# Half-precision output products, and one index search per head instead of two, in a kernel that joins attention with product-key experts

## The chip, the cores and the metric

The kernel runs on one core of one Trainium2 chip. The metric is device time in microseconds, from a median of runs; before the change it is 1775.51 us (three runs, 1774.38 to 1776.06). Beside it stands one execution under the hardware profiler, from which all other times here are taken.

## The reference

The input x has 2048 tokens of 512 numbers. After a layer norm two branches are computed from the same rows and added to x.

```python
q = (xn @ wq).reshape(B, S, 32, 16)         # 32 heads of 16
k = xn @ wk; v = xn @ wv                    # one key and one value head for all
p = softmax(q @ k.T * 16 ** -0.5)
branch_a = concat_heads(p @ v) @ wo         # wo: 512 x 512

q = einsum("nd,dhc->nhc", xn, w_q)          # 32 heads, two halves of 128
s1 = einsum("nhd,ed->nhe", q[..., :128], k1)   # 64 scores of the first half
s2 = einsum("nhd,ed->nhe", q[..., 128:], k2)   # 64 scores of the second half
i1, i2 = the two best of s1, of s2          # by score, with their places
top_s, top_e = the two best of the four sums s1 + s2; expert = 64 * i1 + i2
g = softmax(top_s)
act = gelu(einsum("nd,nhkd->nhk", xn, u[top_e]))
branch_b = einsum("nhk,nhk,nhkd->nd", g, act, v[top_e])
out = x + branch_a + branch_b
```

## The kernel before

The work is written out by hand, engine by engine, in one long order. A start of some 110 us norms and transposes x, forms queries, keys and values of the attention, and splits the weights into a half-precision number and a half-precision remainder, so that one product of single precision becomes three half-precision ones (high by high, high by low, low by high; the list is `TERMS`). Then 256 steps follow, `d` = 0 to 255. A step is eight score products, four exponentials on ACT (line 458) and 16 products with the values (line 468) of the attention; into its gaps a generator, `score_thread`, puts the other branch, and a planner says how much.

The expert branch handles the 16 row tiles of 128 tokens in four groups of four. Groups 0 and 1 are *sparse*: for each of the 512 slots (tile, head and choice) POOL gathers 128 rows of u and v from memory (line 1194), DVE takes the dot product with xn (line 1206), ACT the tanh, and DVE adds the weighted row of v (line 1241). Groups 2 and 3 are *dense*: one-hot tables turn the chosen experts into gate matrices, and all 4096 experts are multiplied through on PE (lines 930 and 1072). Both need the search. An *item* is one tile of 128 tokens by four heads: twelve half-precision products (line 702) leave 512 scores in PSUM, eight half-heads of 64. For each half-head DVE finds the eight largest (line 715) and then their places (line 717, in the chip two instructions: a load of the eight values and the find). There are 128 items. Four items make a `batch`, which picks the two best sums, the expert numbers (on POOL, line 761 on) and the gates.

In time the order is: items of group 0 while the expert weights are made (`wp_make`: products, norms in `wp_factors`, transposes, splits), from step 0; items of two eighths of group 1 and of group 2, to about step 60; the one-hot tables of group 2 and its dense sums, to about step 130; the remaining items of group 1 and those of group 3, to about step 180; the tables and dense sums of group 3, to the end. The slots run beside all this.

Two numbers set the pace. Each piece of generator work states a cost in microseconds of PE (`UNIT` = 0.235 for a half-precision product), and a step runs the generator until the sum reaches its share of `FILL`. And `pos` counts slots: so many dot products may be done by a step, by a rate that depends on the stage (`dense_on`):

```python
aim = done0 + (FILL - done0) * (d + 1) / half if d < half else 1e6
pos += (2.5 if len(IDX) < NC * TPH else 2.3 if 0 <= d - since < 20 else 1.75, 0, 0.25, 1.5, 0.5)[dense_on[0]]
```

In the dense sums the rate is 2.6 up to step 191 and after that whatever remains, divided by the steps that remain.

The attention's result leaves like this. Every 16 steps a pair of units ends; its rows are divided by their sums (`pair_tail`, line 517) and kept as `on`. When four pairs of a query block are there, `block_out` multiplies 128 rows with wo: four single-precision products (line 568), then one DVE addition to the row's sum (line 572). It runs for three of the four query blocks, four row blocks each, at steps chosen by `out_ready`, and states a cost of 3.6. The last query block has code of its own at the end (`last_out_a`, `last_out_b`). wo is loaded before each query block by `load_wo`, into buffers lent for it. One guard stands between the start and the steps (line 384): each engine loads a flag and skips a slow path.

DMA transfers are issued by SP's queue in its order, but for the gathers, which POOL issues, and some of the last stores. Work of a step goes through lists: `on_act` puts a function into the next step's ACT work, `behind` what DVE does after it, `store` what SP issues in a later step.

## Time and profile before

| | us |
|---|---|
| median of three runs | 1775.51 |
| the profiled execution, whole | 1775.3 |
| its span, first to last instruction | 1773.3 |
| PE busy | 1687.8 (95%) |
| DVE busy | 1593.0 (90%) |
| ACT busy | 1329.7 (75%) |
| POOL busy | 680.2 (38%) |
| TensorE's granted clock, mean | 0.995 |

In rows of a timeline stand start, length, engine, line, operation, and the tiles as out<-in. An operation's length covers its latency; the next may start before it ends, so a rate is read from start to start. PE is the matrix engine, PEld its weight loads, SPq an instruction that SP's queue issues. A matrix product in single precision appears as two passes. In groups of instructions the columns after the bar are busy time, the mean of one in ns, and the idle time of the engine just before, with what ended it; in lists of waits they are total, times, and the longest.

### The profile page before, as it was taken

To read this page: it belongs to the slowest core of one execution; us is meant where nothing else is said; L and a number is where in the kernel's file an instruction comes from. 1 tells how busy PE (TensorE), PEld (TensorE's weight loads), DVE (VectorE), ACT (ScalarE), POOL (GpSimd) and SP (SyncE) were. 2 spreads that over 40 slices of the span, in tenths; PEclk is the share of its full clock that TensorE was granted. 3 is DMA by queue.
4 is the path that set the end of the run, shared out by engine and by line. 5 is a ranking of instruction groups with operands and counts; after the bars stand their busy time and mean duration, and the time that the engine had idled before them with its cause. 6 is when DMAs were issued, how large, how long until landed. Compare 5 with 4: busy or idle time off the path is not lost.

```text
span 1773.3 us, 35071 instructions
## 1 busy us (share of the span) xinstructions
PE 1687.8 (95%) x11070; PEld 597.5 (34%) x11070; DVE 1593.0 (90%) x6367; ACT 1329.7 (75%) x1793; POOL 680.2 (38%) x893
## 2 busy tenths in 40 slices
PE   7989998999998889999999999999998899999998
PEld 3433333333333333333333333333333333333332
DVE  7748898999999977999999999999999779999995
ACT  6467787877776988888988666666679877777774
POOL 1024454445542003444444445445520125455450
PEclk9999999999999999999999999999999999999999
DMA  7378879999773469999999977767544779999994
GB/s 272 120 251 313 273 267 309 303 323 336 256 257 103 158 220 280 330 334 337 332 338 360 357 264 240 236 222 230 177 126 137 235 235 330 327 311 345 321 311 146
DMA packets 257272, 470.97 MB, mean 266 GB/s; under 512 B 107316, under 2 KB 118596, under 8 KB 257084
## 3 DMA queue, kind: packets, MB, share of 16 engines
q0 software_dynamic: 73728, 268.47, 44.1%
q1 hardware_dynamic: 182940, 199.59, 34.7%
q8 instruction: 87, 1.43, 0.3%
q14 instruction: 101, 0.83, 0.1%
q10 hardware_dynamic: 416, 0.66, 0.1%
HBM read 407.36 MB, written 56.39 MB: 262 GB/s over the span
## 4 chain that ended last, share of the span: by engine, by line
PE 52%; DVE 30%; ACT 6%; issue 3%; DMA 1%; POOL 0%; SPq 0%; ACTq 0%; DVEq 0%; POOLq 0%
PE pv L468 16%; PE sc L451 9%; PE pout L1072 8%; PE pact L930 7%; DVE i L717 7%; PE psc L702 6%; DVE xa L1241 5%; DVE m L715 5%; DVE g L1206 4%; ACT pt L458 4%; DVE oh L988 3%; PE pwo L568 2%; PE pw L647 1%; DVE obs L991 1%; DVE obs L990 1%
## 5 line engine op out<-in xcount | busy, mean ns | idle before, releaser
L458 ACT ACTIVATE pt<-sc 128x1024 f32<-128x1024 f32 x1024 | 990.4, 1025 | 316.9 <-PE sc L451 269.8
L1194 POOL DMA_INDIRECT g<-in_uv_dram,idx x512 | 550.1, 1074 | 862.2 <-DVE xa L1241 395.3
L468 PE MATMUL pv<-pt,vaug 128*32 128x512 f32 x4096 | 495.0, 601 | 0.0
L1241 DVE SCALAR_TENSOR_TENSOR xa<-g,w,xa 128x512 f32<-128x512 f32 x512 | 374.0, 746 | 0.1
L702 PE MATMUL psc<-wk,xt 128*128 128x512 f16 x1536 | 356.4, 380 | 7.2 <-DVE wk L663 4.7
L451 PE MATMUL sc<-qa,kaug 64*128 64x512 f16 x2048 | 323.5, 383 | 36.3 <-ACT pt L458 29.5
L1206 DVE CUSTOM_DVE_ANT_0 g<-g,xa 128x512 f32<-128x512 f32 x512 | 334.6, 683 | 14.5 <-DMA g<-in_uv_dram,idx 14.2
L702 PEld LDWEIGHTS <-xt 128*128 128x128 f16 x1536 | 140.7, 98 | 204.1 <-issue 55.5
L451 PEld LDWEIGHTS <-kaug 64*128 64x128 f16 x2048 | 82.6, 94 | 373.9 <-issue 370.5
L717 DVE FIND_INDEX8 i<-m,psc 128x8 uint32<-128x64 f32 x1024 | 206.6, 224 | 0.0
L468 PEld LDWEIGHTS pv<-pt,vaug 128*32 128x32 f32 x4096 | 107.2, 109 | 253.5 <-issue 253.5
L930 PE MATMUL pact<-xt,wk 128*128 128x512 f16 x768 | 182.6, 383 | 0.0
L1072 PE MATMUL pout<-wk,wd 128*128 128x512 f16 x768 | 175.8, 379 | 0.0
L715 DVE MAX8 m<-psc 128x8 f32<-128x64 f32 x1024 | 146.2, 216 | 6.5 <-PE psc L702 6.2
L1072 PEld LDWEIGHTS <-wd 128*128 128x128 f16 x768 | 73.0, 98 | 92.6 <-issue 8.1
L930 PEld LDWEIGHTS <-wk 128*128 128x128 f16 x768 | 69.1, 98 | 99.9 <-issue 26.7
L988 DVE TENSOR_TENSOR oh<-io,tr 128x2048 f16<-128x2048 f16 x64 | 78.0, 1218 | 4.9 <-PE pg L1026 4.8
L717 DVE MATCH_VALUE_LOAD i<-m,psc 128x8 f32 x1024 | 74.3, 73 | 0.0
L761 POOL CAST fi<-i 128x64 f32<-128x64 uint32 x30 | 7.7, 257 | 145.6 <-DVE i L717 142.0
L1075 DVE SCALAR_TENSOR_TENSOR da<-pout,cols,da 128x512 f32<-128x512 f32 x72 | 53.0, 744 | 5.9 <-PE pout L1072 5.4
L1145 DVE SCALAR_TENSOR_TENSOR gy<-gy,pact 128x512 f32<-128x512 f32 x60 | 40.8, 680 | 17.3 <-ACT gy L1144 17.0
L880 DVE SCALAR_TENSOR_TENSOR wk<-rw,cols,wk 128x512 f16<-128x512 f32 x64 | 47.5, 745 | 6.9 <-ACT wk L877 6.9
(227 smaller groups left out, 1451.9 us busy)
## 6 DMA issues: line engine op xcount, KB each, us to landing
wk<-dw SPq DMA_DIRECT2D x96, 256.0 KB
wqt<-in_wqT_dram SPq DMA_DIRECT2D x32, 512.0 KB
un<-in_uv_dram SPq DMA_DIRECT2D x16, 1024.0 KB
ds<-wk SPq DMA_DIRECT2D x64, 256.0 KB
gates<-dg SPq DMA_DIRECT2D x64, 256.0 KB
wk<-ds SPq DMA_DIRECT2D x64, 256.0 KB
dg<-gst SPq DMA_DIRECT2D x14, 928.0 KB
dw<-wk SPq DMA_DIRECT2D x32, 256.0 KB
```

The source lines that it names most:

```text
L451: nc.tensor.matmul(p[:, b, :], kaug[o:o + 64, kc * P:(kc + 1) * P], QA[u][o:o + 64, i, :], start=True, stop=True)
L458: nc.scalar.activation(PT[u, kc, i], p, AF.Exp, scale=SCALE)
L468: nc.tensor.matmul(PV[u][32 * j:32 * j + 32, :], vaug[:, kc, :], pt[:, b, :], start=kc == 0, stop=kc == 15)
L702: nc.tensor.matmul(p, XT[kk][:, a, j * P:(j + 1) * P], WC[n_][kk][:, bb, :], start=n == 0, stop=n == 11)
L715: nc.vector.max(m8[:, jb, s, :], p[:, s * E:(s + 1) * E])
L717: nc.vector.max_index(i8[:, jb, s, :], m8[:, jb, s, :], p[:, s * E:(s + 1) * E])
L930: nc.tensor.matmul(p, us[:, a, k * P:(k + 1) * P], XT[k][:, c, :], start=n == 0, stop=n == 11)
L988: nc.vector.tensor_tensor(out=oa, in0=num(P), in1=bc(0, tb, P), op=OP.is_equal)
L1072: nc.tensor.matmul(p, wd[0][:, a, j * P:(j + 1) * P], vs[:, c, :], start=n == 0, stop=n == last)
L1194: nc.gpsimd.indirect_dma_start(out=gt, out_offset=None, in_=uv, in_offset=bass.IndirectOffsetOnAxis(ap=IDX[ph, c, ti][:, s:s + 1], axis=0))
L1206: nc.vector.tensor_tensor_reduce(u, u, XN[TPH * ph + ti], scale=1.0, scalar=0.0, op0=OP.mult, op1=OP.add, accum_out=a[:, i:i + 1])
L1241: nc.vector.scalar_tensor_tensor(acc, v, w[:, i:i + 1], acc, op0=OP.mult, op1=OP.add)
```

## The change

**One search per head.** The eight maxima are taken per half-head as before, the first halves first. But they are written into one row of 16 places per head, the second half's from place 6 on, over the two smallest of the first half. So places 0 to 7 hold the six best of the first half and the two best of the second, and one find over the head's 128 columns gives all eight places; for the second half 64 is taken off. If the place of one of the second half's two is below 64, an equal value stood in the first half, and the place is not the one wanted. POOL works that out per batch (`over`), DVE keeps the running maximum (`most`), and near the end it becomes a flag. The whole kernel is written into the program a second time, with the old search (`exact`), behind a branch on that flag.

**Output products from halves.** wo is loaded once more in step 48, its squares summed, scaled by a power of two and split into a half-precision high and low part in steps 50 to 57, and stored; `load_wo` reads these, of the same size in bytes, for three query blocks. `pair_tail` now also splits the pair's rows: the high part on ACT, the low part on DVE. `block_out` makes twelve half-precision products, and the addition to the row sum takes the factor along. The last query block stays in single precision.

**Norms of the expert weights.** `wp_factors` makes one product of four columns and sums them on DVE, where four products of one column were accumulated, and scales on DVE what ACT scaled.

**Slots and pace.** `FILL` is 937.2 and a block costs 2.7. The slots' rate is 2.6 for 2.5 and 2.05 for 1.75.

```diff
-FILL = 948.0
+FILL = 937.2
...
+        nc.vector.tensor_scalar(col(S_O), col(S_WKV), 1.0 / 32.0, None, op0=OP.mult)
...
     def pair_tail(pp):
...
+        rs, ot = RB.pop(pp), OT.pop(pp)
+        if pp > 11:
+            on = late[0].tile([P, 512], F32, name="on", tag="on", bufs=5)
+            nc.vector.tensor_mul(on, ot, rs)
+        else:
+            on = late[0].tile([P, 2, 512], F16, name="on", tag="on", bufs=5)
+            nc.vector.tensor_mul(ot, ot, rs)
+
+            def high():
+                nc.scalar.activation(on[:, 0, :], ot, AF.Copy, scale=col(S_O))
+                behind(lambda: nc.vector.scalar_tensor_tensor(on[:, 1, :], ot, col(S_O), on[:, 0, :],
+                                                              op0=OP.mult, op1=OP.subtract))
+
+            on_act(high)
         ON[pp] = on
...
+    def wo_square(h):
+        junk = big.tile([P, 2, D], BF16, name="junk", tag="wk", bufs=NWK)
+        nc.scalar.activation(junk, NU["wo"][h], AF.Square, accum_out=wo_sums[:, h:h + 1])
...
+    def wo_split(k):
+        raw_, w = NU["wo"][k // 2][:, k % 2, :], wk_tile()
+        nc.scalar.activation(w[:, 0, :], raw_, AF.Copy, scale=col(S_WO))
+        behind(lambda: nc.vector.scalar_tensor_tensor(w[:, 1, :], raw_, col(S_WO), w[:, 0, :],
+                                                      op0=OP.mult, op1=OP.subtract))
+        store(lambda: store(lambda: nc.sync.dma_start(d_wo[:, k], w)))
...
+    def wo_steps(d):
+        if d == 48:
+            wo_raw()
+        if d in (50, 51):
+            on_act(lambda: wo_square(d - 50))
+        if d == 53:
+            wo_factors()
+        if 54 <= d < 58:
+            on_act(lambda: wo_split(d - 54))
...
     def block_out():
...
         for k in range(KC):
-            nc.tensor.matmul(p, ON[4 * m + k][:, j * P:(j + 1) * P], WO[k // 2][:, k % 2, :],
-                             start=k == 0, stop=k == KC - 1)
+            for a, c in TERMS:
+                nc.tensor.matmul(p, ON[4 * m + k][:, a, j * P:(j + 1) * P], WO[k // 2][:, k % 2, c, :],
+                                 start=n == 0, stop=n == 11)
+                n += 1
...
-        behind(lambda: nc.vector.tensor_add(acc, acc, p))
+        behind(lambda: nc.vector.scalar_tensor_tensor(acc, p, col(C_WO), acc, op0=OP.mult, op1=OP.add))
...
     def wp_factors():
...
-        p = xtile("pn")[:, :1]
-        for h in range(4):
-            nc.tensor.matmul(p, ones_f, squares[:, h:h + 1], start=h == 0, stop=h == 3)
+        p = xtile("pn")[:, :4]
+        nc.tensor.matmul(p, ones_f, squares, start=True, stop=True)
         x = small.tile([P, 1], F32, name="xw")
-        nc.scalar.activation(x, p, AF.Copy, scale=col(K2))
+        nc.vector.reduce_sum(x, p, axis=AX.X)
+        nc.vector.tensor_mul(x, x, col(K2))
...
+    SECOND = 8 if exact else 6
...
-        for s in range(8):
-            nc.vector.max(m8[:, jb, s, :], p[:, s * E:(s + 1) * E])
-        for s in range(8):
-            nc.vector.max_index(i8[:, jb, s, :], m8[:, jb, s, :], p[:, s * E:(s + 1) * E])
+        for s in (0, 2, 4, 6, 1, 3, 5, 7):
+            nc.vector.max(m8[:, jb, s // 2, SECOND * (s % 2):][:, :8], p[:, s * E:(s + 1) * E])
+        if exact:
...
+        else:
+            for h in range(4):
+                nc.vector.max_index(i8[:, jb, h, :8], m8[:, jb, h, :8], p[:, h * P:(h + 1) * P])
...
+        if not exact:
+            over = T("over", F32, [P, BT, 4, 2])
+            G_.tensor_scalar(over, fv[:, :, :, 1, :], float(E), -float(E), op0=OP.is_ge, op1=OP.mult)
+            G_.tensor_add(fv[:, :, :, 1, :], fv[:, :, :, 1, :], over)
...
-                    yield 3.6
+                    yield 2.7
...
-                pos += (2.5 if len(IDX) < NC * TPH else 2.3 if 0 <= d - since < 20 else 1.75, 0, 0.25, 1.5, 0.5)[dense_on[0]]
+                pos += (2.6 if len(IDX) < NC * TPH else 2.3 if 0 <= d - since < 20 else 2.05, 0, 0.25, 1.5, 0.5)[dense_on[0]]
...
 def build(nc, tc, args):
-    tile_kernel(tc, *args)
+    with tc.tile_pool(name="met", bufs=1) as met:
+        flag = met.tile([1, 1], I32, name="met")
+        tile_kernel(tc, False, flag, *args)
+        again = nc.values_load(flag[0:1, 0:1], min_val=0, max_val=1)
+        with tc.If(again != 0):
+            tile_kernel(tc, True, None, *args)
```

In the order of the instructions, DVE near step 60, in the search of group 2, before (`m` are the maxima of an item, `i` their places, `psc` its scores, `g` a gathered row, `xa` a row sum):

```order
L715 MAX m_7511<-psc 128x8 x8
L717 MAX_INDEX i_7512<-m_7511,psc 128x8 x8
L1206 ISA g,act<-g,xa 128x512
L1206 ISA act 128x1
L1206 ISA g,act<-g,xa 128x512
L1206 ISA act 128x1
L1241 SCALAR_TENSOR_TENSOR xa<-g,w,xa 128x512
L1215 SCALAR_TENSOR_TENSOR gq<-act 128x4
```

and a few steps earlier in the same group after the change, where wo is being split (`wor` is the loaded wo):

```order
L790 MAX m_6817<-psc 128x8 x8
L797 MAX_INDEX i_6818<-m_6817,psc 128x8 x4
L1297 ISA g,act<-g,xa 128x512
L1297 ISA act 128x1
L1297 ISA g,act<-g,xa 128x512
L1297 ISA act 128x1
L1332 SCALAR_TENSOR_TENSOR xa<-g,w,xa 128x512
L1306 SCALAR_TENSOR_TENSOR gq<-act 128x4
L555 SCALAR_TENSOR_TENSOR wk<-wor,cols,wk 128x512
```

The eight finds of an item have become four; the dot products and sums of the slots stand behind them as they did, and the low part of a piece of wo is new.

On PE at the first output block, just after the tables of group 2, before (`pact` is a dense product, `sc` the attention's scores):

```order
L930 LDWEIGHTS wk
L930 MATMUL pact<-xt,wk 128x512
L568 MATMUL pwo<-wo,on 128x512 x4
L451 LDWEIGHTS kaug
L451 MATMUL sc<-qa_197,kaug 128x512
```

and after the change, the first of twelve such pairs:

```order
L1021 LDWEIGHTS wk
L1021 MATMUL pact<-xt,wk 128x512
L625 LDWEIGHTS on
L625 MATMUL pwo<-wo,on 128x512
L625 LDWEIGHTS on
```

The block stands in the same gap between a dense product and the next scores; four products have become twelve, each with a weight load of its own.

## The prediction

> **What bounds the kernel now.** I read the page's busy shares first, then windows cut at the stages of the program, then the rows of one step, then the waits. The page:

> ```profile
> PE 1687.8 (95%) x11070; PEld 597.5 (34%) x11070; DVE 1593.0 (90%) x6367; ACT 1329.7 (75%) x1793; POOL 680.2 (38%) x893
> ```

> Two engines look full, and the change takes work from both, so the question is which of them sets the time, stage by stage. In the windows (columns: stretch, its length, then busy us and instructions of PE, PEld, DVE, ACT, POOL, then TensorE's granted clock, DMA share, GB/s) 110 to 352 holds the first 32 attention steps with sparse search and expert weights being made, 352 to 558 and 1012 to 1289 are search with gathers, 558 to 645 and 1289 to 1403 the one-hot tables, 645 to 1012 and 1403 to 1720 the dense experts:

> ```profile
> 110.00:352.00 242.00, 226.24 (x1399) 79.65 (x1399) 211.54 (x1083) 193.02 (x284) 106.47 (x136) 0.99 0.85 289
> 352.00:558.00 206.00, 201.91 (x1253) 68.20 (x1250) 202.73 (x1325) 154.80 (x210) 98.52 (x187) 1.00 0.82 277
> 558.00:645.00 87.00, 72.56 (x887) 31.02 (x886) 81.59 (x151) 76.82 (x97) 4.53 (x4) 0.98 0.43 143
> 645.00:1012.00 367.00, 355.35 (x2173) 119.26 (x2172) 332.05 (x796) 304.43 (x414) 145.03 (x132) 1.00 0.97 328
> 1012.00:1289.00 277.00, 276.21 (x1673) 93.01 (x1672) 269.94 (x1671) 174.28 (x212) 141.53 (x229) 1.00 0.69 232
> 1289.00:1403.00 114.00, 100.42 (x1081) 40.69 (x1079) 106.75 (x318) 94.62 (x117) 20.95 (x28) 0.99 0.49 159
> 1403.00:1720.00 317.00, 313.61 (x1913) 105.96 (x1914) 281.70 (x706) 246.83 (x329) 142.47 (x130) 1.00 0.94 306
> ```

> From 1012 to 1289 PE is idle for 0.8 us of 277, and DVE, nearly as full, for 7. PE's clock is 1.00, so nothing is throttled. Since ends of matmuls are modelled, I check in one step, from start to start, that PE is working and not stretched by waiting:

> ```profile
> 1170.26 0.61 PE L451 MATMUL sc<-qa,kaug 64*128 64x512 f16 x4
> 1170.80 1.92 PE L468 MATMUL pv<-pt,vaug 128*32 128x512 f32 x16
> 1172.65 0.61 PE L451 MATMUL sc<-qa,kaug 64*128 64x512 f16 x4
> 1173.19 3.41 PE L702 MATMUL psc<-wk,xt 128*128 128x512 f16 x15
> 1176.54 0.60 PE L451 MATMUL sc<-qa,kaug 64*128 64x512 f16 x4
> ```

> The step is 0.54 + 1.85 + 0.54 + 3.35 = 6.28 us. The 15 half-precision products take 0.223 us each, and nothing lies between the groups. So this "DVE-full" stage is bound by PE, and a step costs 2.93 us plus 0.223 us per half-precision product; how many of these a step gets is set by the plan (FILL). The dense stages are of the same kind: PE idle 11.7 of 367 and 3.4 of 317 us. PE has real idle time only in the first stage (15.8 us) and in the two one-hot stages (14.4 and 13.6 us). The waits say the same:

> ```profile
> ACT pt L458 <- PE sc L451: 269.8, 250, 3.8
> PE sc L451 <- ACT pt L458: 29.5, 57, 1.4
> PE pg L1026 <- DVE obs L991: 9.4, 14, 1.8
> PE psc L702 <- DVE wk L663: 4.7, 4, 2.0
> ```

> and, by groups of instructions (busy, mean ns of one, idle before, and what ended it):

> ```profile
> L660 PE MATMUL pwt<-ident,wt 128*128 128x128 f32 x128 | 19.9, 278 | 5.0 <-DVE i L717 3.0 <-PEq L384 1.4 <-DVE wk L663 0.2
> L955 PE MATMUL ptd<-ident,da 128*128 128x128 f32 x24 | 3.9, 283 | 5.9 <-DVE da L820 3.3 <-DVE da L809 1.4 <-DVE gy L943 1.2
> ```

> ACT waits 269.8 us for PE; PE waits for ACT 29.5 us, and for DVE 9.4 + 4.7 + 3.0 + 5.9 = 23 us in these rows.

> **The change part by part.** *Output products in half precision.* A block was four single-precision products (eight passes in the trace); three of the four query blocks, twelve row blocks, now take twelve half-precision products each.

> ```profile
> 1432.26 3.70 PE L568 MATMUL pwo<-wo,on 128*128 128x512 f32 x8
> 1435.89 0.60 PE L451 MATMUL sc<-qa,kaug 64*128 64x512 f16 x4
> ```

> Before: 1435.89 - 1432.26 = 3.63 us. After: 12 x 0.223 = 2.68. Each saves 0.95 us, and all twelve stand in dense or search stages where PE has no gap: -11.4 us. This is the firm term. The plan agrees: FILL falls by 10.8, which is 12 x (3.6 - 2.7), so every step keeps its share of the other work.

> *The norms of the expert weights* (eight calls) go from four small single-precision products (eight passes) to one (two passes).

> ```profile
> 97.38 1.05 PE L625 MATMUL pn<-squares,ones_f 128*128 128x1 f32 x8
> ```

> Six of eight passes of about 0.12 us go: 0.75 us a call, 6.0 in all. Two calls lie in the start, six in the first stage, which has 15.8 us of PE idle to swallow it. Bounds 0 and -6; I take -2.5. The two DVE operations that replace one of ACT are of 0.1 to 0.2 us.

> *The search.* Before, each of 128 items had eight pairs of load and find over 64 columns; now four over 128. The eight maxima per item stay.

> ```profile
> 1169.95 0.07 DVE L717 MATCH_VALUE_LOAD i<-m,psc 128x8 f32 x1
> 1170.01 0.22 DVE L717 FIND_INDEX8 i<-m,psc 128x8 uint32<-128x64 f32 x1
> 1170.15 0.07 DVE L717 MATCH_VALUE_LOAD i<-m,psc 128x8 f32 x1
> 117.12 0.27 DVE L375 TENSOR_REDUCE prd<-pm 1x1 f32<-1x128 f32 x1
> 115.66 0.69 DVE L308 TENSOR_REDUCE qmax<-pqs 128x1 f32<-128x512 f32 x1 [4.78 <-PE pqs L306]
> ```

> A pair costs 0.20 us from start to start. A find over 128 columns is nowhere in the trace. Lower bound: the same 0.20; upper bound: twice, 0.40. The nearest rows that differ only in columns read are the reductions: (0.69 - 0.27) / 384 = 1.1 ns a column, so 64 more columns cost 0.07 and the pair 0.27. Per item 8 x 0.20 - 4 x 0.27 = 0.52 us, over 128 items 67 us of DVE (between 0 and 102).

> What does it buy? In 1012 to 1289 there are

> ```profile
> 1012.00:1289.00 277.00, 83.67 (x800) 1.00 0.69 232
> ```

> 800 / 16 = 50 items (the view of that one line) in some 43 steps of 6.4 us, 1.2 an item a step: 0.61 us of DVE per step is freed. But the slots take most of it back at once: outside the dense stages the rate rises from 1.75 to 2.05 slots a step.

> ```profile
> L1241 DVE SCALAR_TENSOR_TENSOR xa<-g,w,xa 128x512 f32<-128x512 f32 x512 | 374.0, 746 | 0.1
> L1206 DVE CUSTOM_DVE_ANT_0 g<-g,xa 128x512 f32<-128x512 f32 x512 | 334.6, 683 | 14.5 <-DMA g<-in_uv_dram,idx 14.2
> L880 DVE SCALAR_TENSOR_TENSOR wk<-rw,cols,wk 128x512 f16<-128x512 f32 x64 | 47.5, 745 | 6.9 <-ACT wk L877 6.9
> ```

> A slot is (374.0 + 334.6) / 512 = 1.38 us, with its small operations about 1.6; 0.3 of one is 0.48. With 0.08 for the running maximum and for the low half of a head pair (0.745 us every 16 steps), DVE's step becomes only 0.05 us shorter: it stays almost as full as PE in the search stages, and the relief appears in the last dense stage, where 2.5 slots a step are left instead of 3, about 0.8 us of DVE in a step that PE bounds. So 67 us saved on DVE are worth little: I allow half of PE's waits for the search and for the split queued behind it (3.0 + 4.7), -4 us; bounds 0 and -23, all of PE's waits for DVE.

> *New work for ACT and DVE.* Twelve head pairs get a half-precision copy on ACT and a remainder on DVE; wo is squared (two halves) and split (four pieces) in steps 50 to 57.

> ```profile
> L1136 ACT CAST wd<-gy 128x512 f16<-128x512 f32 x60 | 37.2, 623 | 0.0
> L618 ACT ACTIVATE junk<-wqt 128x1024 bf16<-128x1024 f32 x32 | 33.8, 1059 | 0.0
> L877 ACT ACTIVATE wk<-rw,cols 128x512 f16<-128x512 f32 x64 | 44.2, 727 | 0.0
> L627 ACT ACTIVATE xw<-pn,cols 128x1 f32<-128x1 f32 x8 | 2.1, 260 | 3.0 <-PE pn L625 2.9
> ```

> ACT: 12 x 0.62 + 2 x 1.26 (with 0.2 to read the sum) + 4 x 0.73 - 2.1 = +10.8 us. It is covered by the 269.8 us in which ACT waits for PE, except where two squares meet in one step, since the norms of the experts' rows already put one in each: four exponentials of 0.97, two squares of 1.26, 6.4 us in a step of 6.4. What is late then is the next exponential, and PE waits for its accumulator. I take +2; without any cover it would be +10.8. On DVE the splits add 4 x 0.745 in those steps. SP gets two loads and four stores of wo more, in front of query loads, at a DMA share of 0.82; the later loads of wo keep their bytes. POOL gets three small operations more per batch (about 1 us in 30 batches, POOL is busy 38%).

> *The end.* Every engine now loads a flag and branches behind its last instruction. The trace has one such place, the guard between start and steps:

> ```profile
> 119.07 1.06 PE L660 MATMUL pwt<-ident,wt 128*128 128x128 f32 x8 [1.43 <-PEq L384]
> 119.38 0.15 DVE L1591 COPY mm<-mm 32x1 f32<-32x1 f32 x1 [1.34 <-DVEq L384]
> 1767.94 1.53 SPq L555 DMA_DIRECT2D out_dram<-ft  x2
> ```

> It held the engines 1.4 us. Here the last stores are issued by 1769.5 and the span ends at 1773.3, so part of load and branch runs while these land. Bounds 0 and 4; I take +1.5. [...]

> **Sum.** -11.4 - 2.5 - 4 + 2 + 1.5 = -14.4 us against the profiled span of 1773.3: 1758.9. That execution took 1775.3, 2.0 more than its span, and the median of the runs shown is 1775.5, so the run should take about 1761.

> **The rivals.** (a) *DVE was the bound after all.* The chain of waits gives DVE 30%, and its search lines much of it:

> ```profile
> PE 52%; DVE 30%; ACT 6%; issue 3%; DMA 1%; POOL 0%; SPq 0%; ACTq 0%; DVEq 0%; POOLq 0%
> ```

> Then a good part of the net 50 us of DVE (67 less 17 of new work) comes off: a half, 25, with the 11.4 of PE, gives about 1739. Against it: PE's gapless step at 1170. Chance 0.15.

> (b) *Slower: the find over 128 costs more than a third of a microsecond.* Place: the 75 or so search steps of 352 to 558 and 1012 to 1289, where DVE has no room and now carries 0.3 slot more. Each 0.01 us on a pair is 0.05 us a step there (4.8 pairs). At 0.28 DVE's step is what it was; at 0.34 the 0.3 us a step, 22 us, eat the gain of 14; at 0.40 it is 0.6 x 75 = 45, and the time about 1761 + 45 = 1806, less some PE slack, 1800. For it: no row has this shape. Against: the slope of the reductions. Chance 0.08.

> (c) *Within the noise: PE's gain is eaten by ACT and the end.* If all 10.8 us that ACT gets delay exponentials that PE waits for, the DVE term is nothing and the end costs 4, the sum is -11.4 - 2.5 + 10.8 + 4 = +1: 1776. For it: PE already waits 29.5 us for ACT. Against: ACT's 269.8. Chance 0.12.

> (d) *The second run starts.* If a value of the second half's best two meets an equal one outside the first half's six kept, the whole kernel runs again: twice 1760, about 3520. My own count over the inputs, in double precision, of near pairs scaled to one step of single precision expects 0.007 such meetings. [...] No row here shows two equal values. Chance 0.03, most of it for a flag that is raised by something I haven't counted.

> **How the numbers follow.** The forecast holds 0.62 and its own range is 1750 to 1769 (DVE term -14 to 0, ACT 0 to 5, end 0 to 4, norms -6 to 0, not all at once). The range that should hold 8 in 10 reaches to (a) and to the edge of (c): 1738 to 1774. What can be told from no change is about 0.2%, 3.6 us. Faster by more than that, under 1772: 0.61 + 0.15 + 0.04 of (c) = 0.80. Same: 0.01 + 0.07 of (c) + 0.02 of (b) = 0.10. Slower: 0.01 of (c) + 0.06 of (b) + 0.03 of (d) = 0.10.

> **What would show it.** The block's row at x12 in 2.7 us; the pair at 0.27 from start to start; PE idle under 2 us between some 1000 and 1280 with DVE still over 95%; DVE near 80% in the last dense stage; less idle in the first stage; an end of the span some 1.5 us later behind the last store. I would be wrong if a search step fell clearly under 2.93 + 0.223 per product (the floor was not PE's), if such steps grew while PE idles (rival b), or if PE's waits for the exponentials grew by 10 us (rival c).

## The result, and the profile after

| | before | after |
|---|---|---|
| median, us (19 runs each, side by side) | 1778.76 | 1795.07 |
| lowest and highest | 1774.38, 1796.46 | 1786.10, 1805.35 |
| ratio, 95% interval | | 1.0084 [1.0066, 1.0101] |
| the profiled execution | 1775.3 | 1796.91 |
| its span | 1773.3 | 1795.1 |
| TensorE's granted clock, mean | 0.995 | 0.987 |

The change makes the kernel slower, by 0.84%, where I had forecast 0.8% faster. The page after:

```profile
PE 1679.2 (94%) x11073; PEld 590.3 (33%) x11073; DVE 1549.9 (86%) x5424; ACT 1336.5 (74%) x1805; POOL 716.7 (40%) x983
```

PE has 8.6 us less to do and DVE 43, and the span of the profiled execution is 21.8 us longer: the work went and waiting came. What the products and the finds were to become, they became. The block on PE, and the finds on DVE (rows of the timeline):

```profile
669.40 2.75 PE L625 MATMUL pwo<-wo,on 128*128 128x512 f16 x12
672.09 0.61 PE L454 MATMUL sc<-qa,kaug 64*128 64x512 f16 x4
```

```profile
279.45 0.07 DVE L797 MATCH_VALUE_LOAD i<-m,psc 128x8 f32 x1
279.51 0.28 DVE L797 FIND_INDEX8 i<-m,psc 128x8 uint32<-128x128 f32 x1
279.71 0.07 DVE L797 MATCH_VALUE_LOAD i<-m,psc 128x8 f32 x1
```

A block takes 672.09 - 669.40 = 2.69 us (forecast 2.68), a load and find 0.26 (forecast 0.27). The windows of the stages after (columns as before):

```profile
110.00:356.00 246.00, 220.94 (x1351) 75.44 (x1349) 205.89 (x895) 192.61 (x279) 115.47 (x157) 0.99 0.86 293
...
649.00:1015.00 366.00, 335.06 (x2071) 112.14 (x2071) 318.34 (x733) 294.53 (x402) 139.40 (x123) 0.97 0.94 314
1015.00:1309.00 294.00, 294.00 (x1831) 98.84 (x1829) 279.82 (x1391) 188.92 (x232) 170.34 (x284) 1.00 0.75 253
...
1423.00:1730.00 307.00, 303.15 (x1915) 102.87 (x1914) 253.02 (x612) 238.88 (x316) 119.39 (x110) 1.00 0.87 279
```

The later stages are as forecast: no PE idle from 1015 to 1309, DVE at 82% in the last dense stage. The loss is in the first dense stage, 649 to 1015: PE idle is 30.9 us of 366 (before 11.7 of 367), and its clock is down to 0.97. In the first stage idle time grew as well, from 15.8 to 25.1. By the start of its first exponential, step 128 begins at 984.9 us, before it was 962.5: all of the loss lies ahead of it. The waits:

```profile
ACT pt L461 <- PE sc L454: 309.1, 274, 4.5
PE sc L454 <- ACT pt L461: 54.9, 82, 6.8
ACT on L527 <- DVE ot L524: 16.3, 8, 6.7
PE psc L777 <- DVE wk L721: 11.2, 5, 4.9
PE pg L1117 <- DVE obs L1082: 7.5, 10, 1.3
ACT wk L968 <- DMA rw<-in_ub_dram: 6.9, 2, 6.7
DVE ot L524 <- DMA rsb<-dinv: 6.2, 1, 6.2
```

PE's waits for exponentials grew from 29.5 us to 54.9, while ACT's own waiting for PE grew too: ACT has time, but not then. Two rows are new. At eight of the twelve head pairs ACT's copy `on` waits for DVE's multiplication, 16.3 us together, and once a piece of `ub` (the expert weights u as the dense stage loads them, into the buffer `rw`) that ACT is to split comes 6.7 us late. The two largest stops of PE, stretches in which it does nothing, follow these two. The first, at 694 (PE; DVE; ACT; SP):

```profile
691.67 2.76 PE L625 MATMUL pwo<-wo,on 128*128 128x512 f16 x12
700.24 0.68 PE L454 MATMUL sc<-qa,kaug 64*128 64x512 f16 x2 [5.81 <-ACT pt L461]
```

```profile
697.22 0.69 DVE L524 TENSOR_TENSOR ot<-ot,rsb 128x512 f32<-128x512 f32 x1 [6.20 <-DMA rsb<-dinv]
```

```profile
697.95 0.72 ACT L527 ACTIVATE on<-ot,cols 128x512 f16<-128x512 f32 x1 [6.72 <-DVE ot L524]
698.58 0.71 ACT L968 ACTIVATE wk<-rw,cols 128x512 f16<-128x512 f32 x1
699.19 3.77 ACT L461 ACTIVATE pt<-sc 128x1024 f32<-128x1024 f32 x4
```

```profile
683.45 0.44 SPq L510 DMA_DIRECT2D dinv<-rc x1
691.18 0.66 SPq L515 DMA_DIRECT2D rsb<-dinv x1
```

The reciprocals are stored at 683.45 and read back, spread, from 691.18 on, when the store has landed; DVE gets them at 697.22. Before the change only DVE waited for such a transfer, 0.8 us in one place:

```profile
DVE on L517 <- DMA rsb<-dinv: 0.8, 1, 0.8
```

Now ACT has work that depends on it, ahead of the next four exponentials in its order, and PE stands for 5.81 us. The second, at 957 (ACT, then SP):

```profile
953.02 0.72 ACT L1237 ACTIVATE gy<-gy,cols 128x512 f32<-128x512 f32 x1
960.44 0.72 ACT L968 ACTIVATE wk<-rw,cols 128x512 f16<-128x512 f32 x1 [6.69 <-DMA rw<-in_ub_dram]
```

```profile
944.34 0.43 SPq L1392 DMA_DIRECT2D xa<-dxn x1
...
945.76 0.74 SPq L1393 DMA_DIRECT2D xa<-in_x_dram x1
...
948.29 4.30 SPq L926 DMA_DIRECT2D rw<-in_ub_dram x1
```

The four loads of row sums and rows (`xa`) for the next group are issued in step 123, in front of the load that ACT waits for, which is issued at 948.29 and lands 12 us later. Before the change they were issued in steps 126 and 127, the first of them here:

```profile
955.93 0.82 SPq L1301 DMA_DIRECT2D xa<-dxn  x1
```

Around both stops the windows show the clock (the figure behind the busy times):

```profile
694.00:697.00 3.00, 0.43 (x2) 0.09 (x1) 0.00 (x0) 0.00 (x0) 1.28 (x2) 0.96 0.94 211
697.00:703.60 6.60, 3.12 (x16) 0.82 (x19) 4.80 (x12) 5.01 (x6) 0.00 (x0) 0.50 0.89 315
703.60:712.00 8.40, 8.40 (x59) 2.61 (x49) 6.64 (x16) 6.99 (x11) 2.14 (x2) 1.00 0.46 113
...
960.00:970.00 10.00, 5.83 (x25) 1.04 (x25) 6.16 (x15) 7.32 (x11) 1.31 (x2) 0.51 0.96 352
```

Behind each stop PE runs at half its clock for 6.6 and some 10 us.

### The profile page after: what moved, and what is told of

Its sections match the earlier page's. It is cut to its first block, busy times and chain, and to the rows that moved or that the text cites. A ratio compares the mean times of both kernels' runs of the same rounds, so it can differ in the third digit from the quotient of the medians.

```text
span 1795.1 us, 34266 instructions
## 1 busy us (share of the span) xinstructions
PE 1679.2 (94%) x11073; PEld 590.3 (33%) x11073; DVE 1549.9 (86%) x5424; ACT 1336.5 (74%) x1805; POOL 716.7 (40%) x983
## 4 chain that ended last, share of the span: by engine, by line
PE 68%; DVE 9%; ACT 9%; issue 4%; DMA 4%; SPq 0%; ACTq 0%; DVEq 0%
PE pv L471 21%; PE psc L777 16%; PE sc L454 12%; PE pout L1163 8%; PE pact L1021 7%; ACT pt L461 6%; DVE xa L1332 2%; PE pwo L625 1%; DVE oh L1079 1%; DVE g L1297 1%; PE pw L705 1%; DMA rw<-in_vb_dram 1%; DMA rsb<-dinv 1%; DVE i L797 1%; DVE m L790 1%
## 5 line engine op out<-in xcount | busy, mean ns | idle before, releaser
L454 PE MATMUL sc<-qa,kaug 64*128 64x512 f16 x2048 | 325.8, 385 | 57.8 <-ACT pt L461 54.9
L797 DVE FIND_INDEX8 i<-m,psc 128x8 uint32<-128x128 f32 x512 | 138.5, 286 | 0.1
L1079 DVE TENSOR_TENSOR oh<-io,tr 128x2048 f16<-128x2048 f16 x64 | 77.9, 1217 | 10.8 <-PE pg L1117 10.0
L1320 DVE SCALAR_TENSOR_TENSOR w<-gth,ga 128x4 f32<-128x4 f32 x128 | 20.7, 161 | 53.6 <-ACT gth L1313 53.5
L841 POOL CAST fi<-i 128x32 f32<-128x32 uint32 x60 | 12.5, 236 | 108.8 <-DVE i L797 106.4
```

Source lines behind the costliest of these rows:

```text
L454: nc.tensor.matmul(p[:, b, :], kaug[o:o + 64, kc * P:(kc + 1) * P], QA[u][o:o + 64, i, :], start=True, stop=True)
L797: nc.vector.max_index(i8[:, jb, h, :8], m8[:, jb, h, :8], p[:, h * P:(h + 1) * P])
L1079: nc.vector.tensor_tensor(out=oa, in0=num(P), in1=bc(0, tb, P), op=OP.is_equal)
```

## The experiments

All ratios are to the kernel before, on the same chip in turn. The groups e1 to e4, e5 to e8, e9 to e12, e13 to e16 and e17 with e18 ran on different chips, so kernels of different groups are compared through these ratios. Five theories of the loss stood against each other. **P**: ACT's copies of the pairs stand in front of exponentials. **N**: the moved norms make PE wait for DVE. **R**: the slots' new rates. **F**: the thinner plan (`FILL` 937.2 and blocks at 2.7), which puts other work into other steps. **C**: the second copy of the kernel in the program.

**e1, e2: the two halves of the change.** e1 has output products and norms with the old search; e2 has the new search alone. Both have the old rates.

```diff
 e1: -        tile_kernel(tc, False, flag, *args)
     +        tile_kernel(tc, True, None, *args)
 e2: pair_tail, load_wo, block_out, wp_factors, FILL, block cost as before; no wo_steps
```

> The output products from halves and the norms by one product, with the old search by half-heads, the old slot rates and no second copy; FILL 937.2. Theory P (the pair's high part stands in ACT's queue behind the transfer of the reciprocals; when that is late, the exponentials are late, PE stalls and its clock is halved for some microseconds): the loss is here, ratio to before 1.003 to 1.010. Theory R (the raised slot rates make transfers and DVE late): no loss here, the twelve blocks' 11 us come out, ratio 0.990 to 0.996. Theory C (the second copy in the program costs): as R.

> One search per head with the second copy and its flag; old output products, old norms, old rates, FILL 948. Theory P: not slower than before, ratio 0.992 to 1.000. Theory R: the same. Theory C: slower, ratio 1.003 to 1.010.

Measured: e1 1.0147 [1.0123, 1.0171], e2 0.9954 [0.9935, 0.9973]. The search is worth 0.5%; the loss came with the rest, and e1 lies above even theory P's range.

**e3, e4: rates back; second copy out.**

```diff
 e3: -   (2.6 if len(IDX) < NC * TPH else 2.3 if 0 <= d - since < 20 else 2.05,
     +   (2.5 if len(IDX) < NC * TPH else 2.3 if 0 <= d - since < 20 else 1.75,
 e4: -        with tc.If(again != 0):
     -            tile_kernel(tc, True, None, *args)
```

> The whole change with the slot rates 2.5 and 1.75 of before. Theory P: as the change itself, ratio 1.005 to 1.010. Theory R: the loss is gone, ratio 0.988 to 0.996. Theory C: as P.

> The whole change without the second copy of the kernel and without loading the flag (the flag is still computed). Theory P and R: as the change, at most 2 us faster for the end, ratio 1.005 to 1.010. Theory C: ratio 0.990 to 0.998.

Measured: 1.0071 [1.0046, 1.0096] and 1.0091 [1.0068, 1.0115]. Neither differs from the change. C falls. R fell here too, which turned out to be too early (e14).

**e5: norms back.**

```diff
-        p = xtile("pn")[:, :4]
-        nc.tensor.matmul(p, ones_f, squares, start=True, stop=True)
+        p = xtile("pn")[:, :1]
+        for h in range(4):
+            nc.tensor.matmul(p, ones_f, squares[:, h:h + 1], start=h == 0, stop=h == 3)
...
-        nc.vector.reduce_sum(x, p, axis=AX.X)
-        nc.vector.tensor_mul(x, x, col(K2))
+        nc.scalar.activation(x, p, AF.Copy, scale=col(K2))
```

> The changed kernel with the norms as before (four matmuls of one column into the pn bank, the reduction by ScalarE with its scale). Its trace has stops of TensorE of 1.5 and 1.4 us at 146 and 171 us that end with the xw reduction on VectorE, and the kernel with the wo part alone has them too (1.4 to 3.1 us). Theory N (the moved norms make TensorE wait for VectorE, and the clock is halved behind each stop): these stops go and the time falls by 5 to 10 us, to a ratio of 1.003 to 1.006. Theory P (ScalarE's new work for the pairs in front of the exponentials) and theory F (the thinner filling): the time stays within 3 us of the changed kernel's, at 1.007 to 1.010, or is 1 to 3 us worse for the 2.5 us of matmuls that come back.

Measured: 1.0130 [1.0093, 1.0168], slower than with the new norms. The stops behind `xw` went (of those the change had, at 146 and 171 us), others of up to 3.9 us stayed in that stage, and N falls: the new norms earn time, by a difference just clear of its uncertainty (0.46%, give or take 0.41).

**e6, e7: the pair's copy on DVE; the pair one step later.** The variable `r` counts half steps, so e7 moves the pair by one step `d`, some 7 us; its expectation, and that of e10, call this two steps.

```diff
 e6: -                nc.scalar.activation(on[:, 0, :], ot, AF.Copy, scale=col(S_O))
     +                nc.vector.tensor_scalar(on[:, 0, :], ot, col(S_O), None, op0=OP.mult)
     -            on_act(high)
     +            behind(high)
 e7: -            if r == 12:
     +            if r == 14:
                      pair_tail(pp - 1)
```

> The changed kernel with the high half of each pair's output made on VectorE, behind the multiplication, in place of ScalarE. Theory P: the stops of TensorE that end with an exponential behind that copy (5.8 us at 694, the one at 288) go, and the time falls by 8 to 15 us, to a ratio of 1.000 to 1.004. Theory N: no change but VectorE's 12 instructions more, 1.008 to 1.010. Theory F: the bunches of other work ahead of the exponentials (2.9 us at 811) stay and so does the time, 1.007 to 1.010.

> The changed kernel with the pair's multiplication, and with it the ScalarE copy, two steps later (about 7 us), so that the spread reciprocals have landed before VectorE and ScalarE come to them. If theory P holds because the copy waits for a late transfer while the exponentials stand behind it: the 6-us wait at 691 to 698 and the 4-us wait at 285 go, ScalarE still does the copy, and the time falls by 6 to 12 us, to 1.002 to 1.005. If P holds because of the copies' own time (12 of 0.7 us) it stays at 1.008. Theories N and F: 1.007 to 1.010.

Measured: e6 0.9979 [0.9961, 0.9996], e7 1.0040 [1.0023, 1.0058]. P holds: taking the copy off ACT is worth 1.05%, near 19 us, for 12 instructions of 0.72 us. In e7 ACT's waits for the multiplication are no longer among the waits listed, and 0.4% comes back, under half of what e6 wins. What remains may be the copies' own place in ACT's order, or work that shifted with that step. Some did shift: in e7's trace ACT waits 16.4 us at five places for pieces of `ub`, where the change has 6.9 us at two (e7's profiled execution was the slowest of thirteen). e7 does not size these two parts.

**e8, e9, e10: the old pace; with the copy on DVE; and the pair one step later as well.**

```diff
-FILL = 937.2
+FILL = 948.0
-                    yield 2.7
+                    yield 3.6
-            spent[0] += 2.7
+            spent[0] += 3.6
```

> The changed kernel with the filling constant 948 and the block's price 3.6 us in the plan, as before the change, so that the mean load of a step is planned as before. Theory F (the thinner plan moves the work of the gates and of the dense stage into the wrong steps): the time falls by 8 to 15 us, to 1.000 to 1.004. Theories P and N: within 4 us of the changed kernel's, 1.006 to 1.011.

> Two of the edits that each won time, together: the pairs' high half on VectorE (1.05% against the changed kernel alone) and the plan's constant and block price as before (0.4% alone). If ScalarE's copies and the thinner plan are two causes, the gains add and the ratio is 0.993 to 0.996, as good as the search alone (0.9954) with the blocks' 11 us on top of part of the loss. If the old pace only helped by moving the copies away from the exponentials, it adds nothing: 0.997 to 1.000.

> As the kernel with both edits, and the pair's multiplication two steps later as well. If VectorE's wait for the spread reciprocals (4 to 6 us at a time, ahead of other work in its order) still costs TensorE something once ScalarE is out of it, another 3 to 6 us: 0.990 to 0.993. If only ScalarE's share of that wait mattered, the same as without it within 2 us.

Measured: e8 1.0043 [1.0021, 1.0066], e9 1.0015 [0.9995, 1.0036], e10 1.0092 [1.0062, 1.0123]. e9 is slower than e6 and e10 than e9: e9 lies above both of its expectations, and e10 went the other way. e8 wins 0.4%, a little less than theory F asks. Edits that win one at a time do not add. The traces of e9 and e10 show large stops of PE (5.69 us at 902 and 4.86 at 950 in e9; 3.93 at 821 and 6.16 at 934 in e10), and at each ACT waits for a late piece of `ub` ahead of the exponentials. The one at 950 is in step 123, next to that of the change; the other three are in other steps.

**e11, e12: the norms beside the search; ACT's copy beside the search.** e11 is e2 with the norms of the change. In e12, e2 gets only this, for the first twelve pairs:

```diff
-            nc.vector.tensor_mul(on, ot, rs)
+            nc.vector.tensor_mul(ot, ot, rs)
+            on_act(lambda: nc.scalar.copy(on, ot))
```

> The kernel with the search alone (0.9954) and the norms moved as in the change; nothing of the output products. The changed kernel with the norms put back was 0.5% slower (1.013 against 1.008), so if the parts add: 0.990 to 0.993. If the norms pay only beside the split of wo in the same steps, 0.994 to 0.997; theory N (they cost TensorE waits on VectorE) would say 0.998 to 1.000.

> The disputed piece by itself: the kernel with the search alone, in which VectorE multiplies the first 12 pairs in place and ScalarE copies each (128x512) where the changed kernel makes the high half; products, norms, plan and wo as before the change. Theory P (ScalarE's order behind VectorE's multiplication, in front of the exponentials): 10 to 18 us worse than the search alone, 1.001 to 1.006. If what mattered was ScalarE's time only (12 of 0.7 us with 270 us of waits beside it): within 3 us, 0.994 to 0.997.

Measured: e11 0.9930 [0.9905, 0.9956], e12 0.9973 [0.9950, 0.9996]. The norms are worth another 0.2% and the copy alone costs 0.2% here; neither is clear of the noise (the intervals overlap). It is not the 1% of e6, though ACT waits 10.2 us at five pairs for the multiplication: the price of the copy depends on what stands in the same steps.

**e13: copy on DVE and old rates; e14, e15: rates, or plan, put into e11.** The edits are those above.

> The changed kernel with the pairs' high half on VectorE (0.9979 alone) and the gathers' rates 2.5 and 1.75 as before (1.0071 alone, 0.1% under the changed kernel). With the new rates the accumulators' tiles of the next phase are loaded at step 123, beside the qa loads, and the raw half of ub lands late: a 4.5 to 7-us stop at 945 to 968 in every kernel with the new rates. If the collision comes from the rates, this stop is gone here and the ratio is 0.993 to 0.996; if the lost time only moves to another step, 0.997 to 1.000.

> The kernel with search and norms (0.993) with the gathers' rates 2.6 and 2.05 of the change and nothing else. If the rates alone bring the collision of transfers at step 123, 6 to 9 us worse, with the stop there: 0.996 to 0.999. If the collision needs the other pace of the output blocks too: 0.992 to 0.994.

> The kernel with search and norms (0.993) with the plan's constants of the change (937.2 and 2.7 us a block), though its blocks still take 3.6 us; rates as before. If the thinner plan is a cause of its own, 5 to 12 us worse, 0.996 to 1.000, with stops of 2 to 6 us behind exponentials between 600 and 1000 us; if it is not, 0.991 to 0.995.

Measured: e13 0.9998 [0.9979, 1.0017], e14 1.0002 [0.9983, 1.0021], e15 1.0009 [0.9987, 1.0032]. So the rates alone take away all that e11 had won, and the thinner plan alone does too. (Two kernels with the new rates, e4 and e10, lack the stop that e13's expectation gives to every one of them.) In e14 steps 120 to 127 take 7.0 us longer than in e11, with the stop of the change (ACT, then SP):

```profile
945.90 0.72 ACT L950 ACTIVATE wk<-rw,cols 128x512 f16<-128x512 f32 x1 [4.78 <-DMA rw<-in_ub_dram]
```

```profile
934.31 0.54 SPq L1374 DMA_DIRECT2D xa<-dxn x1
...
935.87 0.43 SPq L1375 DMA_DIRECT2D xa<-in_x_dram x1
936.40 0.38 SPq L908 DMA_DIRECT2D rw<-in_ub_dram x1
...
940.72 3.94 SPq L908 DMA_DIRECT2D rw<-in_ub_dram x1
```

ACT waits for the load of 936.40, right behind the four of `xa`; it lands 9.4 us later. In e11 the four loads are issued 13 us later, in steps 126 and 127, and ACT waits for no piece of `ub`:

```profile
947.66 0.83 SPq L1374 DMA_DIRECT2D xa<-dxn x1
```

A faster rate lets POOL reach the next group's first gathers three steps earlier, and `gather` issues those loads. They meet the loads of `ub` in a stage whose DMA share was already 0.97. They are not the only delay: just before them SP's queue stood 5.3 us, at the last load of queries (`qa`), for a piece of `gates`; and no run moves the four loads alone. Nor are the 7.0 us all that e14's trace lost: its span is 22.0 us longer than e11's (its profiled execution was the slowest of twelve), and 11.9 of these lie in steps 0 to 63, not traced to a cause. In e15 the stop is elsewhere (steps 112 to 119, 7.5 us):

```profile
884.30 0.72 ACT L950 ACTIVATE wk<-rw,cols 128x512 f16<-128x512 f32 x1 [6.28 <-DMA rw<-in_ub_dram]
```

That load was issued at 875.63 and landed 8.6 us later, no longer than such loads take in e11's dense stage (27 loads, 3.6 to 8.8 us). It left late: SP's queue had stood 5.5 us, again at the last load of `qa` for a piece of `gates`; at that place of e11 it stands 1.1 us. e15 plans for blocks of 2.7 us and has blocks of 3.6, so it may overstate the plan's part. Putting the rates back in e3 and e13 did not show the rates' part, with the thinner plan left in them: they have no stop at 950, but one of 3.55 us at 728 (e3) and of 5.00 us at 720 (e13), behind a late piece of `ub` too. Such waits of ACT are what these kernels share: 4.1 to 16.4 us in every trace with the new rates or the thinner plan, none listed in those of before, e2, e11, e12 and e18.

**e16: the clock by itself.** e11, with ACT held at eight steps of the stage without PE idle:

```diff
+            if 140 <= d < 180 and d % 5 == 0:
+                on_act(hold_act)
+    def hold_act():
+        for _ in range(16):
+            nc.scalar.activation(held_in, held_in, AF.Copy, scale=1.0)
```

> The clock by itself: the kernel with search and norms (0.993), in whose dense stage, where TensorE has no idle time, ScalarE is held at eight places five steps apart by 16 small activations (128x64, about 4 us together, their result unused) ahead of the exponentials. TensorE should then stand still some 1 to 3 us at each place. If a stop costs only its own length: 8 to 24 us more, 0.998 to 1.006, and a granted clock of 1.00 in the stage. If the clock is halved for 3.4 us behind each stop of 2 us or more, as 50 of the 64 such stops in the earlier traces had it: half of 3.4 us more for each, some 14 us, 1.004 to 1.015, and the granted clock of the stage under 0.97.

Measured: 1.0069 [1.0040, 1.0097], 1.4% over e11, some 25 us. A hold, 16 activations of 256 ns, takes 4.6 us from its first start to its last end, and TensorE's longest stop behind one was 0.95 to 2.2 us. Window 1036 to 1286 of e11, and of e16:

```profile
1036.00:1286.00 250.00, 250.00 (x1513) 84.19 (x1512) 225.10 (x1167) 157.88 (x193) 141.43 (x260) 1.00 0.66 216
```

```profile
1036.00:1286.00 250.00, 233.23 (x1381) 77.77 (x1379) 209.64 (x1076) 173.52 (x297) 129.35 (x228) 0.99 0.63 207
```

The ratio fits the second expectation, its mechanism doesn't: PE's idle time, 16.8 us in this window, is most of it, and only two of the eight stops were followed by a halved clock (3.4 us each). So 4.6 us of ACT ahead of the exponentials cost some 3 us of the kernel each time (25 us by the runs, 22 by the traces' steps 136 to 183, over eight), in a stage where ACT is busy 63% of the time.

**e18, e17: the whole change with the plan's three numbers as before; and the pairs' copy on DVE as well.** The edits are those of e3, e8 and e6.

> The whole change (search, norms, output products in halves, pairs on ScalarE, second run) with its three numbers of the plan as before: constant 948, block price 3.6 us, rates 2.5 and 1.75. With the rates alone put into the kernel of search and norms 0.993 became 1.0002, with the thinner plan alone 1.0009. If the plan's numbers carry the loss and the output products themselves are worth their 11 us less the copies' 3: 0.988 to 0.993. If the products cost whatever the plan is: 1.001 to 1.006.

> As the kernel with the whole change and the plan's numbers as before, and the pairs' high half on VectorE. If ScalarE's copies cost 3 us in the old plan, as beside the search alone (0.9973 against 0.9954): 2 to 5 us less than with ScalarE, 0.986 to 0.991. If, as in the changed plan, they cost 18 us: 10 or more us less. No better than search and norms (0.993): then the output products earn nothing in this program.

Measured: e18 0.9984 [0.9964, 1.0005], e17 0.9902 [0.9874, 0.9931]. e17 has a median of 1762.74 us against 1779.51 and is faster than both kernels. e18 lies between its two expectations; the copies cost 0.8%, some 15 us, in the old plan too, as e17's second alternative has it (10 or more) and not its first (2 to 5). The tile `on` in e18 (what ended the idle time of its engine: us, times):

```profile
  DVE ot L524: 15.0, 6
```

In e17 no such row is left. At the pairs the waiting is now DVE's alone, 7.2 us at two of them for `rsb`, and PE's waits for exponentials are 34.7 us:

```profile
ACT pt L461 <- PE sc L454: 311.7, 283, 3.7
PE sc L454 <- ACT pt L461: 34.7, 61, 5.4
...
DVE ot L524 <- DMA rsb<-dinv: 7.2, 2, 4.8
```

One stop behind a late piece of `ub` stands even here, at 890 (PE, then ACT; e17's profiled execution was the slowest of six); e18's trace has none of that kind:

```profile
895.81 0.61 PE L454 MATMUL sc<-qa,kaug 64*128 64x512 f16 x2 [5.39 <-ACT pt L461]
```

```profile
893.40 1.44 ACT L968 ACTIVATE wk<-rw,cols 128x512 f16<-128x512 f32 x2 [5.55 <-DMA rw<-in_ub_dram]
```

Together these runs make a table of ratios, by what the kernel does and by which of the plan's numbers are new:

| | rates and pace old | rates new | pace new (the thinner plan) | both new |
|---|---|---|---|---|
| search and norms | 0.9930 (e11) | 1.0002 (e14) | 1.0009 (e15) | not run |
| whole change, copies on DVE | 0.9902 (e17) | 1.0015 (e9) | 0.9998 (e13) | 0.9979 (e6) |
| whole change, copies on ACT | 0.9984 (e18) | 1.0043 (e8) | 1.0071 (e3) | 1.0084 (after) |

In every row one new number alone costs 0.6 to 1.1%, and both together cost about as much as one (0.8 and 1.0%). In every column the copies cost more on ACT than on DVE, by 0.3 to 1.05%; at 0.3% (e8 against e9) the difference is not clear of the noise.

## Why the prediction was wrong

Taken apart in the order e2, e11, e17, e18, after, the ratios give, in us of some 1780 (each difference has an uncertainty of about 3 to 7, so the pieces of 4 and 5 us are not clear of zero):

| piece | ratio from, to | us | forecast |
|---|---|---|---|
| search, flag, second copy | 1, 0.9954 | -8 | -4 search, +1.5 end |
| norms | 0.9954, 0.9930 | -4 | -2.5 |
| output products, with the pairs' copies and splits on DVE | 0.9930, 0.9902 | -5 | -11.4 |
| the pairs' copies on ACT instead | 0.9902, 0.9984 | +15 | in +2 |
| rates and pace | 0.9984, 1.0084 | +18 | 0 |

In another order the pieces would be sized otherwise, as the table above shows.

- **Two steps failed.** The first: "It is covered by the 269.8 us in which ACT waits for PE", by which new work on ACT was priced at +2. That sum is made of 250 waits of at most 3.8 us, and ACT works in order (its rows at 697.95 to 699.19): what stands ahead of four exponentials delays them whatever ACT waits elsewhere. I added up the copies' time (12 of 0.62, really 0.72) and not what they wait for. My "without any cover it would be +10.8" was no upper bound, since the copy holds ACT until a transfer lands (6.7 us at its longest).
- The second: "The plan agrees: FILL falls by 10.8 ... so every step keeps its share of the other work", and with it the rates, which I weighed on DVE's time only. The numbers decide when transfers are issued, too. The window of 645 to 1012 in my own prediction has a DMA share of 0.97; I read PE and DVE in that row and not this figure. In e14, where the rates alone are new, four loads leave three steps earlier and the steps there take 7 us more; how much of that is these loads and how much SP's wait before them stays open, and so does the way in which pace and rates work on each other.
- **Rival (c)** named the mechanism, exponentials delayed by ACT's new work, and its sign that PE's waits for exponentials grow by 10 us: they grew by 25.4. It was given +1 for the sum and 0.12, with its price capped at ACT's busy time.
- *Output products*: the block's time held to 0.01 us. Of the 11.4 us, 5, give or take 7, reach the end when the pairs' copies are on DVE (e17). DVE's additional work and the split of wo are in that figure; I haven't separated them.
- *Norms*: -4, give or take 6, against -2.5, inside the bounds. But "less idle in the first stage" was wrong for the change as a whole; two of its stops there (1.48 and 1.40 us) end with the new `xw` reduction.
- *Search*: the pair's time held, DVE stayed at 95% in the stage 1015 to 1309, and some 72 us off DVE's finds (128 items of 8 x 0.20 less 4 x 0.26) were worth about 8. Rivals (a) and (b) fall, and (d) did not occur.
- *The end*: the last store was issued 5.4 us before the end of the span, now 8.4:

```profile
1786.70 1.53 SPq L610 DMA_DIRECT2D out_dram<-ft x2
```

  3.0 us more, twice what I took and inside 0 to 4. No run shows what the upper bound of 4 rests on, which rival (c) takes as the price of the end; the runs showed these 3.0 us. The time from TensorE's last product to the end was 4.8 us before the change and is 7.9 after it; it is 5.7 in the two kernels without the branch and copy (e1 and e4) and 7.3 to 8.8 in all others with them, but e4's runs do not differ from the change's.

That e17 stands 16.8 us under the kernel before, where I forecast 14.4 for the change, is no success of the sum: its terms were other ones.

## What to carry to other kernels

A sum of idle time on an engine is no cover for new work (here 269.8 us of it, for twelve copies of 0.72 us); look at the one place in the engine's order where the new instruction will stand, at what it waits for, and at who is behind it. Where a hand-set plan places transfers in a stage whose DMA share is near 1 (here 0.97 before and 0.94 after), change the work first and leave the plan's numbers, then move them one by one, since gains of single edits did not add here. And compare two kernels step by step: the traces of e2, e11 and e12 agree to 0.1 us in most groups of eight steps, so a loss of 7 us stands out in the group where it arises.

## What the runs showed of the hardware

Half clock adds up to 17.1 us before the change and 41.0 after (20 to 1760 us), and since at half clock at most half of the time is lost, up to 12 of the 21.8 us by which the span grew are an effect of stops on the clock (an estimate from these sums; where PE stands still it loses nothing by the clock). Of the whole span after the change it is at most 20.5 us of 1795, 1.1%, by the same estimate.

With 256 steps that run the same program, I had also not expected single edits to spread so far: putting the old pace back made e8 0.4% faster than the change and e9 0.4% slower than e6.
